# The first batch of an attention-then-MoE kernel: another order of its steps, and unused matmuls on TensorE between them

## The chip, the cores and the metric

The kernel runs on one core of a Trainium2 chip. A core has five engines, each with its own in-order instruction stream: TensorE (PE, matmul; PEld is its weight load), VectorE (DVE), ScalarE (ACT), GpSimd (POOL) and SyncE (SP, which here only issues DMAs). They wait for one another through semaphores. Matmuls read SBUF and write PSUM, which has eight banks per partition. The metric is the device time of one execution in microseconds (us); lower is better. Runs of one kernel are compared by their median.

## The reference

```python
rms = np.sqrt(np.mean(x * x, axis=-1, keepdims=True) + 1e-06)      # rmsnorm(x, g)
return x / rms * g
...
q_n, k_n = (rmsnorm(q, g_q), rmsnorm(k, g_k))
scores = scale * np.matmul(q_n, k_n.transpose(0, 1, 3, 2))
scores = scores - np.max(scores, axis=-1, keepdims=True)
attn = np.exp(scores)
attn = attn / (np.sum(attn, axis=-1, keepdims=True) + 1e-09)
return np.matmul(attn, v)
...
x = attn_out.transpose(0, 2, 1, 3).reshape(B * S, H * D)
h = x @ w_in
g = np.maximum(0.01 * h, h)
return g @ w_out
```

q, k and v are 8 x 12 x 448 x 64 in fp32 (batch, heads, sequence, head dimension); w_in is 768 x 2048, w_out 2048 x 768. The output is 3584 x 768.

## The kernel before, in words

**Units.** A unit is four heads of one batch, so there are 24 units (`NU`), three to a batch (`NQ`). A unit's sequence of 448 is cut into seven steps (`NS`) of 64 keys, for two heads (`a`) by two heads (`r`).

**Preparation of a unit.** `load` puts q and k into raw tiles through SP (three buffers), `load_v` puts v into one of five tiles through GpSimd's queue, which also carries the weights (`load_w_in`, `load_w_out`). Squares come from ScalarE (`prep_sq`, L126) or GpSimd (`prep_sqp`, L130), q times g from GpSimd (`prep_qg`, L134), the sums of squares from VectorE (`prep_ssq`, L139), the inverse root from ScalarE (`prep_rinv`, L144 and L145), the normalised tiles from VectorE (`prep_norm`, L151). The transposed q and k (`qkT`) come from 14 TensorE transposes and two copies out of PSUM (`prep_tr`, L159 and L160) for units 0 to 4, and from a DMA transpose on SP's queue (`prep_trd`, L163) from unit 5 on. `gate` (L229) is a small GpSimd copy that waits for the normalised k and so holds GpSimd's later work.

**Scores and exponentials.** `qk` computes the scores of a step with four matmuls into one of two two-bank slots (`sT`, L179); `ex` applies the exponential on ScalarE (L198, for step 0 from `score0` L196). All rows of a unit share one shift per partition, taken from the maximum of step 0: `shift_max` (L211 to L218, VectorE) finds the maximum and writes it on a diagonal, `shift_mm` (L223 to L226) spreads it by a matmul with ones and makes `eb`, the bias of the exponentials. So a unit's first exponential waits for scores, maximum, diagonal, matmul, maximum and `eb` in turn.

**Z and PV.** In the first batch `zsum` (L238) sums the exponentials by 28 matmuls with ones, `pv` (L309) multiplies them with v by 28 matmuls; `zinv` (L295 to L300) makes the inverse of Z as exp(-ln Z) on ScalarE, `xmul` (L318) multiplies on VectorE into `xt`, the MoE's input. `zsum_slot` puts Z into one of the two score slots. The remaining accumulators, transposes and small banks take turns in four PSUM banks (`aux`): a new tile waits until the readers of the one four tiles earlier are done.

**MoE.** `moe1` (L324, L326) computes one of 16 blocks of h from six matmuls and applies the leaky ReLU on ScalarE; `moe2` (L339, L343) computes the output. They are put in a queue when a batch's attention is complete, and `fill` deals them out between the steps of the later units, from unit 3 on. The order is written out by hand (a manual schedule): what stands first in the program stands first on its engine.

**The head.** The first batch (units 0 to 2) has no MoE work to lay between its steps. Ahead of unit 0 stand 60 unused matmuls (`warm`, L401), 128 x 128 with ones, in two groups. The loop over `u in range(3)` (L457 to L523) then does, for each unit: `ex` of step 0; `zinv` of the unit before; norm of the next unit; sum of squares of the one after; loads; steps 1 and 2, 3 and 4, 5, 6 with their exponentials; transposes of the next unit; step 0 of the next unit and its shift; Z and PV. Unit 2 does Z and PV of steps 0 to 4 together after step 6, then those of steps 5 and 6.

Of the kernel before, what the change touches and what calls it, by code (L numbers as in the profile page):

```python
# [8 lines left out]
FP32 = mybir.dt.float32  # L9
# [9 lines left out]
def kernel(  # L19
# [11 lines left out]
    nc = tc.nc  # L31
# [3 lines left out]
    NS = 7  # L35
    P = 128
# [18 lines left out]
    def aux(shape, dtype, name):  # L55
        return psum.tile(shape, dtype, tag="aux", bufs=4, name=name)
# [36 lines left out]
    st = {}  # L93
# [111 lines left out]
    def shift_max(u):  # L205
# [11 lines left out]
        s["dg"] = small.tile([P, P], FP16, tag="dg", name="dg")  # L217
        nc.vector.tensor_tensor(s["dg"], ident16, s["spare"][:, 511:512].broadcast_to([P, P]), op=ALU.mult)  # L218

    def shift_mm(u):  # L220
        s = st[u]
        pb = aux([P, 512], FP32, "pb")
        nc.tensor.matmul(pb[:, 0:P], onesp, s["dg"], start=True, stop=True)  # L223
        nc.vector.tensor_reduce(s["spare"][:, 510:511], pb[:, 0:P], axis=AXL.X, op=ALU.max)
        s["eb"] = small.tile([P, 1], FP32, tag="eb", name="eb")
        nc.vector.tensor_scalar(s["eb"], s["spare"][:, 510:511], -1.0, DELTA, op0=ALU.mult, op1=ALU.add)  # L226

    def gate(u):
        nc.gpsimd.tensor_copy(gate_t, buf(u, "n16")[:, 1, NS - 1, 1, D - 1:D])  # L229
# [166 lines left out]
    K0, K1 = (0, 1), (1, NS)  # L396
    VV = ((ALL, vcopy),)

    def warm(n):
        for x in range(n):  # L400
            nc.tensor.matmul(wbank[:, 0:P], onesp, onesp, start=True, stop=True)  # L401

    with tc.manual_schedule():
        nc.scalar.dma_start(grow[:, 0], g_q[None, :])
        nc.scalar.dma_start(grow[:, 1], g_k[None, :])
        nc.scalar.preload_act_table_set("natural_log_exp_and_others")
        load(0)
        load(1)
        load(2)
        gps = aux([P, 512], FP32, "gps")  # L410
        wbank = aux([P, 512], FP32, "warm")
        warm(32)
        nc.vector.scalar_tensor_tensor(grow[:, 0], grow[:, 0], 0.125, grow[:, 1], op0=ALU.mult, op1=ALU.mult)
        nc.tensor.matmul(gps[:, 0:D], one32, grow[:, 0], start=True, stop=True)
        warm(28)
        prep_sq(0, CA, (0,))
        prep_sq(0, CB, (0,))
        acopy(ggb, gps[:, 0:D])
        prep_sq(0, ALL, (1,))
        prep_qg(0, nc.gpsimd, CA)  # L420
        prep_qg(0, nc.gpsimd, CB)
        prep_ssq(0, CA, (0,))
        prep_ssq(0, CB, (0,))
        prep_rinv(0, (0,))
        prep_ssq(0, ALL, (1,))
        prep_rinv(0, (1,))
        prep_sq(1, ALL, (0,))
        load_v(0)
        load_v(1)
        prep_norm(0, CA, (0,))  # L430
        prep_norm(0, CB, (0,))
        prep_tr(0, 0, ((CA, acopy), (CB, acopy)))
        prep_norm(0, K0, (1,))
        prep_norm(0, K1, (1,))
        tpk = aux([P, NS, P], FP16, "tp")

        def trk(c, copy):
            for x in range(*c):
                nc.tensor.transpose(tpk[:, x, :], buf(0, "n16")[:, 1, x].rearrange("p a d -> p (a d)"), ident16)
            copy(buf(0, "qkT")[:, 1, c[0]:c[1]], tpk[:, c[0]:c[1]])  # L440

        trk(K0, vcopy)
        prep_ssq(1, ALL, (0,))
        qk(0, STEPS[0])
        prep_sq(1, ALL, (1,))
        trk(K1, acopy)
        prep_sq(2, ALL, (0,))
        load(3)
        gate(0)
        prep_qg(1, nc.gpsimd)  # L450
        prep_sqp(2, (1,))
        shift_max(0)
        shift_mm(0)
        load_w_in(0, 1024)
        load_v(2)

        for u in range(3):  # L457
            n = u + 1
            ex(u)
            if u == 0:  # L460
                prep_ssq(n, ALL, (1,))
                prep_rinv(n)
            else:
                zinv(u - 1)
            prep_norm(n)
            prep_ssq(u + 2)
            load(u + 4)
            gate(n)
            prep_qg(u + 2, nc.gpsimd)
            prep_sqp(u + 3)  # L470
            load_v(u + 3)
            if u == 0:
                load_w_in(1024, 1024)
            if u == 1:
                for f in range(2):
                    load_w_out(8 * f, 8)
            qk(u, STEPS[1])
            ex(u)
            if u > 0:
                prep_tr(n, 0, VV)  # L480
                prep_tr(n, 1, VV)
                xmul(u - 1)
            qk(u, STEPS[2])
            ex(u)
            if u == 0:
                prep_tr(n, 0, VV)
            qk(u, (5,))
            ex(u)
            prep_rinv(u + 2)
            if u == 0:  # L490
                prep_tr(n, 1, VV)
                qk(u, (6,))
                ex(u)
                score0(n)
                shift_max(n)
                shift_mm(n)
            elif u == 1:
                score0(n)
                shift_max(n)
                qk(u, (6,))  # L500
                ex(u)
                shift_mm(n)
            else:
                qk(u, (6,))
                ex(u)
            if u < 2:
                zsum_slot(u)
                pv(u)
            else:
                st[u]["zt"] = [aux([P, 512], FP32, "zt") for r in range(2)]  # L510
                zsum(u, 0, 5)
                pv(u, 0, 5)
                qk(n, STEPS[0])
                zsum(u, 5, NS)
                pv(u, 5, NS)
                zinv(u)
                shift_max(n)
                xmul(u)
                push_moe1(0)
                push_moe2(0)  # L520
                queue.pop(0)[1]()
                shift_mm(n)
                ex(n)  # L523

        for u in range(3, NU):
            for d in range(4):
                if d > 0 or u > 3:
                    qk(u, STEPS[d])
                    if d == 0:
                        shift_max(u)  # L530
                        if narrow(u - 1):
                            pv_slot(u - 1)
                            zcol(u - 1)
                            shift_mm(u)
                            pv_out(u - 1)
                            zcol_sum(u - 1)
                        else:
                            zsum_slot(u - 1)
                            pv(u - 1)
                            shift_mm(u)  # L540
                            zinv(u - 1)
                    ex(u)
                jobs = []

                def job(fn, *args):
                    jobs.append(lambda: fn(*args))

                if d == 0:
                    if u == 3:
                        prep_norm(4)  # L550
                        gate(4)
                    elif narrow(u - 1):
                        job(zcol_inv, u - 1)
                    else:
                        xmul(u - 1)
                    if u + 4 < NU:
                        job(load, u + 4)
                    if u + 2 < NU:
                        prep_qg(u + 2, nc.gpsimd)
                    if u + 3 < NU:  # L560
                        load_v(u + 3)
                    if 6 < u < NU - 2:
                        for ti in range(2):
                            job(prep_sq, u + 2, ALL, (ti,))
                if d == 1 and u > 3 and narrow(u - 1):
                    xmul_pool(u - 1)
                if fed(u, d) and u > 3:
                    push_moe1(u // NQ - 1)
                    push_moe2(u // NQ - 1)
                if u < 6 and d == 2:  # L570
                    prep_sqp(u + 3)
                if u == 3 and d == 1:
                    for ti in range(2):
                        prep_tr(4, ti, VV)
                if u + 2 < NU:
                    if d == 1:
                        for ti in range(2):
                            job(prep_ssq, u + 2, ALL, (ti,))
                    if d == 2:
                        job(prep_rinv, u + 2)  # L580
                        for ti in range(2):
                            job(prep_norm, u + 2, ALL, (ti,))
                        job(prep_trd, u + 2)
                fill(u, d, jobs)
        zsum_slot(NU - 1)
        pv(NU - 1)
        zinv(NU - 1)
        xmul(NU - 1)
        push_moe1(B - 1)
        push_moe2(B - 1)  # L590
        while queue:
            queue.pop(0)[1]()
# [28 lines left out]
```

## Time and profile before

| | us |
|---|---|
| median of six runs | 449.02 |
| the six runs | 449.88, 449.85, 447.74, 448.19, 450.05, 447.77 |
| profiled execution | 447.45 |
| its span, first to last instruction | 445.7 |

The page of the profile gives each engine's busy time in the span: PE 417.9 us (94%), ACT 306.6 (69%), DVE 215.9 (48%), POOL 148.2 (33%). The mean granted TensorE clock is 0.984. In lists of instructions a line gives start, duration, engine, source line, operation, tiles (out<-in), and in brackets how long the engine had been idle and who ended the wait. A wait for several events is put down to the last. `PEclk` is the granted clock, 1.00 for full speed. The span's first 48 us are the head and the start of unit 3.

### The profile page before, as it was taken

How to read it: one execution, taken by the hardware profiler on the slowest of the kernel's cores; microseconds unless marked ns; L12 is line 12 of the kernel's file. 1: busy time of each engine (PE TensorE's matmuls, PEld its weight loads, DVE VectorE, ACT ScalarE, POOL GpSimd, SP SyncE). 2: the span in 40 equal slices, each digit the busy share in tenths (PEclk: the TensorE clock that was granted, in tenths of full speed). 3: DMA queues.
4: the chain of work that ended last, by engine and by line, in shares of the span. 5: the costliest groups of instructions: out<-in, count | busy, mean ns of one | idle time of the engine just before them, and what ended most of it. 6: DMA issues, size and time to landing. Idle time of an engine off the chain costs nothing.

```text
span 445.7 us, 8599 instructions
## 1 busy us (share of the span) xinstructions
PE 417.9 (94%) x3608; PEld 212.7 (48%) x3608; DVE 215.9 (48%) x320; ACT 306.6 (69%) x458; POOL 148.2 (33%) x102
## 2 busy tenths in 40 slices
PE   5668999999999999999999999999999999999995
PEld 5234444444445544454445544454455544555563
DVE  5886664875435735555345734545446521120021
ACT  5888788577886498787886598776995677634300
POOL 5896563643413413523512413423511110100000
PEclk9599999999999999999999999999999999999999
DMA  8999999589547855587558784586443550211022
GB/s 276 241 249 254 225 157 181 162 170 215 117 129 143 212 162 96 135 214 145 125 139 109 197 210 65 144 203 153 131 79 78 124 107 1 60 54 37 0 72 71
DMA packets 67979, 62.81 MB, mean 141 GB/s; under 512 B 37477, under 2 KB 62821, under 8 KB 67941
## 3 DMA queue, kind: packets, MB, share of 16 engines
q1 hardware_dynamic: 57664, 50.47, 45.6%
q0 software_dynamic: 10272, 11.80, 17.6%
q8 instruction: 28, 0.46, 0.4%
q14 instruction: 11, 0.08, 0.0%
q10 hardware_dynamic: 4, 0.00, 0.0%
HBM read 45.61 MB, written 11.01 MB: 127 GB/s over the span
## 4 chain that ended last, share of the span: by engine, by line
PE 75%; ACT 16%; DVE 5%; DMA 2%; issue 1%; SPq 0%; DVEq 0%; ACTq 0%
PE op L339 31%; PE hps L324 24%; ACT et L198 7%; PE sT L179 7%; PE sT L309 5%; PE zc L255 3%; ACT sq L126 3%; ACT gt L326 3%; DMA rq<-in_q_dram 2%; PE sT L238 1%; DVE n L151 1%; ACT zs L278 1%; PE pb L223 1%; PE pv L309 1%; ACT zs L277 1%
## 5 line engine op out<-in xcount | busy, mean ns | idle before, releaser
L198 ACT ACTIVATE et<-sT,eb 128x896 f16<-128x896 f32 x166 | 158.9, 1006 | 37.5 <-PE sT L179 26.4
L324 PE MATMUL hps<-xt,win 128*128 128x448 f16 x768 | 153.8, 353 | 1.3 <-DVE xt L318 1.0
L339 PE MATMUL op<-wout,gt 128*128 128x384 f16 x896 | 153.8, 326 | 0.4 <-ACT gt L326 0.4
L339 PEld LDWEIGHTS <-gt 128*128 128x128 f16 x896 | 84.7, 98 | 66.5 <-issue 12.5
L324 PEld LDWEIGHTS <-win 128*128 128x128 f16 x768 | 72.0, 98 | 72.1 <-issue 10.3
L289 POOL TENSOR_TENSOR xt<-x,rz 128x896 f16<-128x896 f32 x19 | 39.6, 2084 | 182.3 <-DMA rz<-zs 98.3
L326 ACT ACTIVATE gt<-hps 128x448 f16<-128x448 f32 x128 | 67.0, 546 | 21.4 <-PE hps L324 20.9
L343 DVE COPY ost<-op 128x384 f32<-128x384 f32 x56 | 31.2, 556 | 95.2 <-PE op L339 91.3
L134 POOL TENSOR_TENSOR qg<-rq,ggb 128x896 f32<-128x896 f32 (+2 forms) x25 | 60.3, 2415 | 45.6 <-DVE n L151 41.5
L139 DVE TENSOR_REDUCE ssq<-sq 128x14 f32<-128x896 f32 (+2 forms) x49 | 50.3, 1060 | 30.3 <-ACT sq L126 30.3
L179 PE MATMUL sT<-qkT 64*64 64x448 f16 x664 | 54.2, 372 | 10.6 <-ACT et L198 9.6
L151 DVE TENSOR_TENSOR n<-qg,rinv 128x896 f16<-128x896 f32 (+2 forms) x25 | 27.4, 1100 | 41.4 <-issue 26.7
L267 ACT COPY x<-sT 128x896 f32<-128x896 f32 x19 | 17.2, 906 | 38.4 <-PE sT L309 38.4
L179 PEld LDWEIGHTS <-qkT 64*64 64x64 f16 x672 | 16.2, 105 | 47.4 <-issue 43.0
L216 DVE TENSOR_REDUCE sT<-sT 128x1 f32<-128x896 f32 x22 | 24.1, 1094 | 27.2 <-PE sT L179 27.2
L151 DVE TENSOR_TENSOR n<-rk,rinv 128x896 f16<-128x896 f32 (+2 forms) x25 | 33.2, 1330 | 0.0
L309 PE MATMUL sT<-et,vt 64*64 64x448 f16 x532 | 28.4, 349 | 0.3 <-ACT et L198 0.3
L309 PEld LDWEIGHTS <-vt 64*64 64x64 f16 x672 | 20.2, 107 | 10.9 <-issue 0.9
L126 ACT ACTIVATE sq<-rq 128x896 f32<-128x896 f32 (+2 forms) x19 | 17.0, 901 | 2.0 <-DMA rq<-in_q_dram 2.0
L106 POOL DMA_DIRECT2D vt<-in_v_dram x24 | 18.3, 763 | 0.0
L255 PE MATMUL zc<-et,onesr 128*32 128x448 f16 (+1 forms) x304 | 16.1, 332 | 0.0
L126 ACT ACTIVATE sq<-rk 128x896 f32<-128x896 f32 x17 | 16.0, 939 | 0.1
(60 smaller groups left out, 197.5 us busy)
## 6 DMA issues: line engine op xcount, KB each, us to landing
rq<-in_q_dram SPq DMA_DIRECT2D x24, 448.0 KB, 4.8
rk<-in_k_dram SPq DMA_DIRECT2D x24, 448.0 KB, 5.8
out_dram<-ost SPq DMA_DIRECT2D x56, 192.0 KB, 2.8
rz<-zs SPq DMA_DIRECT2D x38, 224.0 KB, 3.5
vt<-in_v_dram POOLq DMA_DIRECT2D x24, 224.0 KB, 5.1
win<-in_moe_w_in_dram POOLq DMA_DIRECT2D x8, 384.0 KB, 14.3
wout<-in_moe_w_out_dram POOLq DMA_DIRECT2D x2, 1536.0 KB, 27.0
qkT<-n SPq DMA_TRANSPOSE x19, 4.0
```

What stands on the lines that cost most here:

```text
L126: nc.scalar.activation(buf(u, "sq")[:, ti, :, c[0]:c[1]], raw[u][ti][:, :, c[0]:c[1]], AF.Square)
L134: eng.tensor_tensor(buf(u, "qg")[:, :, c[0]:c[1]], raw[u][0][:, :, c[0]:c[1]], ggb[:, None, None, :].broadcast_to([P, 2, n, D]), op=ALU.mult)
L139: nc.vector.tensor_reduce(buf(u, "ssq")[:, ti, :, c[0]:c[1]], buf(u, "sq")[:, ti, :, c[0]:c[1]], axis=AXL.X, op=ALU.add)
L151: nc.vector.tensor_tensor(buf(u, "n16")[:, ti, c[0]:c[1]].rearrange("p s a d -> p a s d"), src[:, :, c[0]:c[1]], buf(u, "rinv")[:, ti, :, ...
L179: nc.tensor.matmul(banks[a][64 * r:64 * r + 64, 0:S].rearrange("p (t x) -> p t x", t=NS), kT(u, r, a, t), qT(u, r, a), start=True, stop=True)
L198: nc.scalar.activation(s["et"][:, t], sT[:, :, 0:S], AF.Exp, bias=s["eb"], scale=1.0)
L289: nc.gpsimd.tensor_tensor(xts[b][:, g], s["x32"], s["rz"], op=ALU.mult)
L309: nc.tensor.matmul(s["pv"][r][64 * a:64 * a + 64, 0:S], vts[u % NV][64 * r:64 * r + 64, a, t], s["et"][64 * r:64 * r + 64, t, a], start=(t ...
L324: nc.tensor.matmul(hps[:, 0:S], win16[:, kt // 2, kt % 2, ts(ft, P)], xt[:, kt // 2, kt % 2], start=(kt == 0), stop=(kt == KT - 1))
L326: nc.scalar.activation(gt[:, ft, ds(S * (b % 2), S)], hps[:, 0:S], AF.Prelu, bias=0.0, scale=1.0, alpha=0.01)
L339: nc.tensor.matmul(op2[:, 0:HC], gt[:, ft, ts(t, P)], wout16[:, ft, ds(HC * half, HC)], start=(ft == 0), stop=(ft == FT - 1))
L343: nc.vector.tensor_copy(ost[0][:, ds(HC * half, HC)], op2[:, 0:HC])
```

## The change

- `shift_mm`'s PSUM bank can be taken earlier (`shift_bank`), and `warm` writes into any bank; 12, 20 and 6 unused matmuls go into the second quarter of the shift banks of units 0, 1 and 2, ahead of the shift matmul. 16, 12 and 6 more stand behind steps 1, 2 and 3 of unit 0.
- The loop over the first three units is written out. A unit's end (`close`, units 0 and 1) is Z, the exponential of step 0 of the next unit, its step 1 of QK, PV, and `zinv`. Before, step 1 of QK stood behind PV, with step 2.
- Unit 0: transposes of unit 1 stand together behind step 4, the second copied by ScalarE (before: apart, behind steps 4 and 5, both copied by VectorE). `prep_rinv(2)` moves from behind step 5 to behind step 6.
- Unit 2: Z and PV are accumulated as steps come: 0 to 2 after the exponential of step 4, 3 after step 5, 4 after step 6, then step 0 of unit 3, then 5 and 6 (before: 0 to 4 after step 6). `prep_rinv(4)` moves behind step 6, `prep_ssq(4)` behind the transposes of unit 3 and `xmul(1)`.

From unit 3 on the program is the same.

```diff
+    def shift_bank(u):
+        st[u]["pb"] = aux([P, 512], FP32, "pb")
+
     def shift_mm(u):
         s = st[u]
-        pb = aux([P, 512], FP32, "pb")
+        if "pb" not in s:
+            shift_bank(u)
+        pb = s["pb"]
...
-    def warm(n):
+    def warm(n, bank):
         for x in range(n):
-            nc.tensor.matmul(wbank[:, 0:P], onesp, onesp, start=True, stop=True)
+            nc.tensor.matmul(bank[:, P:2 * P], onesp, onesp, start=True, stop=True)
...
         shift_max(0)
+        shift_bank(0)
+        warm(12, st[0]["pb"])
         shift_mm(0)
         load_w_in(0, 1024)
         load_v(2)
 
-        for u in range(3):
...
+        def feed(u):
             load(u + 4)
-            gate(n)
+            gate(u + 1)
             prep_qg(u + 2, nc.gpsimd)
             prep_sqp(u + 3)
             load_v(u + 3)
...
+        def trn(u, ti, copy):
+            prep_tr(u, ti, ((ALL, copy),))
+
+        def sums(u, t0, t1):
+            zsum(u, t0, t1)
+            pv(u, t0, t1)
+
+        def close(u):
+            n = u + 1
+            zsum_slot(u)
+            ex(n)
+            qk(n, (1,))
+            pv(u)
+            zinv(u)
+
+        ex(0)
+        prep_ssq(1, ALL, (1,))
+        prep_rinv(1)
+        prep_norm(1)
+        prep_ssq(2)
+        feed(0)
+        load_w_in(1024, 1024)
+        wb = aux([P, 512], FP32, "warm")
+        qk(0, (1,))
+        ex(0)
+        warm(16, wb)
+        qk(0, (2,))
+        ex(0)
+        warm(12, wb)
+        qk(0, (3,))
+        ex(0)
+        warm(6, wb)
+        qk(0, (4,))
+        ex(0)
+        trn(1, 0, vcopy)
+        trn(1, 1, acopy)
+        qk(0, (5,))
+        ex(0)
+        qk(0, (6,))
+        ex(0)
+        prep_rinv(2)
+        score0(1)
+        shift_max(1)
+        shift_bank(1)
+        warm(20, st[1]["pb"])
+        shift_mm(1)
+        close(0)
+
+        prep_norm(2)
+        prep_ssq(3)
+        ex(1)
+        feed(1)
+        for f in range(2):
+            load_w_out(8 * f, 8)
+        qk(1, (2,))
+        ex(1)
+        trn(2, 0, vcopy)
+        trn(2, 1, vcopy)
+        xmul(0)
+        qk(1, (3, 4))
+        ex(1)
+        qk(1, (5,))
+        ex(1)
+        prep_rinv(3)
+        score0(2)
+        shift_max(2)
+        qk(1, (6,))
+        ex(1)
+        shift_bank(2)
+        warm(6, st[2]["pb"])
+        shift_mm(2)
+        close(1)
+
+        prep_norm(3)
+        ex(2)
+        feed(2)
+        qk(2, (2,))
+        ex(2)
+        trn(3, 0, vcopy)
+        trn(3, 1, vcopy)
+        xmul(1)
+        prep_ssq(4)
+        qk(2, (3,))
+        ex(2)
+        qk(2, (4,))
+        ex(2)
+        st[2]["zt"] = [aux([P, 512], FP32, "zt") for r in range(2)]
+        sums(2, 0, 3)
+        qk(2, (5,))
+        ex(2)
+        sums(2, 3, 4)
+        qk(2, (6,))
+        ex(2)
+        prep_rinv(4)
+        sums(2, 4, 5)
+        qk(3, STEPS[0])
+        sums(2, 5, NS)
+        zinv(2)
+        shift_max(3)
+        xmul(2)
+        push_moe1(0)
+        push_moe2(0)
+        queue.pop(0)[1]()
+        shift_mm(3)
+        ex(3)
```

The removed lines of the loop are those of L457 to L523 above.

More of the change, by code (lines that the diff above doesn't have):

```diff
@@ L411 @@
         wbank = aux([P, 512], FP32, "warm")
-        warm(32)
+        warm(32, wbank)
         nc.vector.scalar_tensor_tensor(grow[:, 0], grow[:, 0], 0.125, grow[:, 1], op0=ALU.mult, op1=ALU.mult)
         nc.tensor.matmul(gps[:, 0:D], one32, grow[:, 0], start=True, stop=True)
-        warm(28)
+        warm(28, wbank)
         prep_sq(0, CA, (0,))
@@ L455 @@
         load_v(2)
-        for u in range(3):
[L458 to L466, printed above, removed]
+        def feed(u):
             load(u + 4)
-            gate(n)
+            gate(u + 1)
             prep_qg(u + 2, nc.gpsimd)
@@ L471 @@
             load_v(u + 3)
[L472 to L523, printed above, removed]
+        def trn(u, ti, copy):
+            prep_tr(u, ti, ((ALL, copy),))
```

## The prediction

> **What bounds the kernel now.** I read the busy shares first, then five stages by the clock stretches, then ScalarE's list up to the first MoE matmuls, then the chain of waits and the DMA answers.
>
> ```profile
> PE 417.9 (94%) x3608; PEld 212.7 (48%) x3608; DVE 215.9 (48%) x320; ACT 306.6 (69%) x458; POOL 148.2 (33%) x102
> ```
>
> TensorE bounds the kernel as a whole, but not its head. The stages say where it doesn't (columns: stretch, length, busy time of PE, PEld, DVE, ACT, POOL, then PEclk, DMA share, GB/s):
>
> ```profile
> 7.50:11.20 3.70, 0.82 (x12) 0.67 (x12) 2.68 (x6) 2.46 (x6) 3.08 (x5) 1.00 1.05 392
> 11.20:21.50 10.30, 7.00 (x53) 3.04 (x52) 8.68 (x12) 9.42 (x14) 9.14 (x10) 0.50 1.10 240
> 21.50:31.70 10.20, 6.12 (x103) 3.47 (x100) 9.32 (x16) 7.83 (x11) 10.20 (x11) 1.00 1.13 249
> 31.70:35.10 3.40, 2.80 (x29) 1.27 (x32) 2.94 (x8) 2.50 (x6) 2.98 (x4) 0.50 1.14 238
> 35.10:48.00 12.90, 9.74 (x143) 5.60 (x136) 7.70 (x14) 10.72 (x16) 6.23 (x5) 1.00 1.13 247
> ```
>
> Up to 48 us ScalarE, VectorE and GpSimd are fuller than TensorE; from 49 to 61.3 us TensorE is busy for 11.75 of 12.30 us, from 91 to 130 for 38.54 of 39. So a microsecond won in the head moves all that follows, unless something later is tied to a clock of its own. The reader also sees two half-clock stretches, 10.3 and 3.4 us. What the head loses stands in ScalarE's brackets:
>
> ```profile
> 19.55 1.01 ACT L198 ACTIVATE et<-sT,eb 128x896 f16<-128x896 f32 x1 [0.28 <-PE sT L179]
> 24.27 1.16 ACT L196 ACTIVATE et<-s,eb 128x448 f16<-128x448 f32 x2 [2.34 <-DVE eb L226]
> 35.35 0.92 ACT L295 ACTIVATE rz<-sT 128x896 f32<-128x896 f32 x1 [1.06 <-PE sT L238]
> 43.77 0.54 ACT L299 ACTIVATE rz<-zt 128x448 f32<-128x448 f32 x1 [0.67 <-PE zt L238]
> 47.06 0.54 ACT L326 ACTIVATE gt<-hps 128x448 f16<-128x448 f32 x1 [1.10 <-PE hps L324]
> ```
>
> These are 5.45 us of gaps; elsewhere between 13 and 48 us ScalarE runs through. The 2.34 us is the shift chain of unit 1 (two copies, scores, two maxima, diagonal, matmul, eb); the 1.06 us is Z of unit 1 at half clock:
>
> ```profile
> 23.57 1.52 PE L238 MATMUL sT<-et,ones 64*64 64x448 f16 x28
> 32.50 2.80 PE L238 MATMUL sT<-et,ones 64*64 64x448 f16 x28
> ```
>
> **The change part by part**, against the profiled execution: 447.45 us, span 445.7 and 1.75 around it.
>
> *Unused matmuls.* 72 are added (12+16+12+6+20+6). Their price is in the first microseconds:
>
> ```profile
> 1.16 3.49 PE L401 MATMUL warm<-onesp 128*128 128x128 f16 x32 [1.16 <-DVE onesp L67]
> 4.95 1.74 PE L401 MATMUL warm<-onesp 128*128 128x128 f16 x28
> ```
>
> 109 ns each in the first 3.4 us, 62 ns after: slow and full clock. The first 12 go between the last six transposes (from 11.64) and the shift matmul, in the half-clock stretch: 18 x 0.109 from 11.64 is 13.60, where the shift matmul starts at 13.28 now. So eb and ex of unit 0 come later by **+0.32** (0 if the clock is full there, 0.5 if each pair drains first; I take the issue row). The 16 start about 14.2. The busy stretch that 18.07 to 21.48 is now (after it the clock is full) then lies at 11.2 to 14.65, so the clock should be full from 14.65. The 16 end about 15.4, where step 2 waits for ex 0 anyway; the 12 and 6 (0.75 and 0.37 us) fit in the 0.92 us that each ex takes. The 20 (1.24 us) run while VectorE does 1.9 us of maxima and diagonal, the 6 before dg of unit 2. If that cover went, each group would cost its own length.
>
> *Unit 0's end.* Both transposes now follow step 4 and the second copy goes from VectorE (0.62) to ScalarE (0.80 us for 768 columns, so 0.93). VectorE is back to back from rinv at 15.68 through norms and sums to the copies' end at 21.02; with one copy less, scores of unit 1 start 0.62 sooner, and take 0.38 instead of 0.56 at full clock: **-0.80**. ScalarE pays the 0.93 and rinv of unit 2 (0.57), moved behind ex 6, inside its 2.34 us gap: its work ends at about 23.0, eb comes at 23.8. Cover gone (a gap below 1.5 us), they would be on the path. Norm 2 on VectorE is next behind rinv 2 and needs it at 23.7. So ex of unit 1 starts 0.48 sooner, 23.8.
>
> *Second QK step before PV.* Four matmuls (0.19 us of issue) ahead of 28. ScalarE goes from rz (26.27, 0.95 long) into ex at 27.12 with no gap now, and at 37.16 likewise: **0**; PV comes 0.2 later, its reader xmul waits for the tp copies long after.
>
> *Unit 1.* VectorE and ScalarE run without a gap from eb, so all moves by 0.48 to Z of unit 1. Does the clock fall there? Cut into single microseconds, the granted clock changes at about 11.24, 21.48, 31.72 and 35.14, all multiples of 3.41 us apart, so I count TensorE's busy time in such windows. In 28.31 to 31.72 TensorE was busy 1.57 us and the clock fell after it; in 38.55 to 41.96 it was busy 1.82 and kept it. The same steps plus 6 fillers (0.37) make about 1.95. I take full clock: Z 1.5 us, done at 33.3 before ScalarE frees at 33.85, and the **-1.06** gap goes. Bounds: 0 and -1.06. The Trainium skill, "TensorE: Matmul & The Clock Gate", HAM oscillation, speaks against this: its rule is to avoid TensorE gaps longer than about 3.4 us. The longest gap before 31.7 is 0.52 us and the clock fell all the same, so the trace decides; by the rule the fillers would buy nothing here and the sum would lack this term: 447.1 instead of 446.0.
>
> *Unit 2.* rinv of unit 4 moves behind ex 6, so Z's last step (0.57) runs beside it: from ex at 37.16 to 43.77 is 6.61 us now, 6 x 0.92 + 0.57 = 6.09 after: **-0.52**. ssq of unit 4 moves behind copies and xmul of unit 1 on VectorE: done about 40.3, needed 41.5. But the first Z group now stands before step 5 in TensorE's queue, and its banks are those that xmul 1 reads (ends about 38.3): 12 Z and 12 PV matmuls (0.048 each, 1.1 us) then hold step 5 until 39.35, ready for ScalarE at 39.75 instead of 39.45: **+0.30** (0 to 1.2, if xmul slips). V of unit 2, issued 16.58 and landed after 16.1 us, is there by 32.7.
>
> *Queues.* The loads on SP and GpSimd stand in the same order as before; only the time shifts. GpSimd runs full from 18.0 to 34.7, its gate waits for norm 1, 0.3 later. w_in's second half lands at 46.5, needed after 50.
>
> *The DMA transpose of unit 5*, the next to be late:
>
> ```profile
> 71.63 0.38 PE L179 MATMUL sT<-qkT 64*64 64x448 f16 x4 [0.29 <-DMA qkT<-n]
> ```
>
> It is issued at 58.56, right after norm 5, and TensorE waits for its landing 13 us later; later ones land in 4.0 to 5.0 us. DMA share is over 1 from 11 to 72 us. If the landing is fixed by the backlog, all the gain goes here; if it moves with its issue, nothing. In 61.5 to 62, beside weights still moving, its queue passed 92 packets in 0.5 us; alone, from 65 to 68, some 170 in 1 us. So sharing doesn't slow it, and an earlier start should carry over: **+0.3** of a possible 1.7.
>
> Sum: 0.32 - 0.80 - 1.06 - 0.52 + 0.30 + 0.3 = -1.46, so 446.0 for such an execution.
>
> **To the median.** The six times are two groups, 447.74 to 448.19 and 449.85 to 450.05; the profiled one belongs to the first, 0.32 under its middle: 446.3. What makes the second group no trace shows; I guess half-clock stretches falling elsewhere, which fillers should shorten, and allow 0.2: **446.5 us**. The same page (What's actually happening) says that the clock's window runs freely and doesn't restart with a kernel; no trace here shows that.
>
> **Rivals.**
> - *The transpose holds the gain.* For it: the saturated share; against: the packet rates. The gain stops at its 0.28: 447.2 to 447.8.
> - *Half clock in unit 1 stays.* 1.95 us may be too little. Loses 1.06: 447.1, with the transpose and the second group 447.0 to 448.3.
> - *Slower: the fillers don't lift the clock in unit 0.* Then steps are held by them: 16 take 1.75 us and 12 take 1.31, QK 0.59; step 3 comes at 18.75 instead of 17.8, step 4 another 0.35 late, 14 transposes 1.53 for 0.87, the shift matmul 0.3, Z 1.3, less the copy's 0.62: +3.3 with the first 0.32. This gives 450.7, without Z 449.4; it decides once the clock stays down past about 18. Against it: 32 in a row lifted the clock after 3.4 us at the start.
> - *No change in effect*: the old gaps reappear as others, 449.
>
> **How the numbers follow.** Main case 0.55 (444.9 to 447.3; the lower end is no DMA loss, no 0.30, first 0.32 zero), transpose 0.14, half clock 0.11, slower 0.10, no change 0.10. Within 0.3% of 449.02, which a measurement can just tell, is 447.67 to 450.37. Faster: 0.55 + most of 0.25 = 0.73; within: 0.18; slower: 0.09. The range leaves out the slower case and half of no change: 444.9 to 449.2.
>
> **What would show it.** PEclk near 1 from 15 us on; ex of unit 1 at 23.8; no gap before rz of unit 1, Z in 1.5 us; rz of unit 2 at 42.0; the sixth matmul of the first MoE group at about 45 (46.68 now); TensorE's wait on qkT near 70 under 0.6. Wrong if 0.50 stands in PEclk after 18 us, if that wait is over 1.5, or if step 5 of unit 2 is over 1 us late.

## The result, and the profile after

The changed kernel takes 445.93 us (median of 22 runs, 443.95 to 447.45) against 449.06 us of the kernel before (46 runs, 447.48 to 450.96). The ratio is 0.9925 with a 95% interval of 0.9913 to 0.9936: 0.75% faster. A later repetition of 12 runs on another chip gave 0.9949 (0.9932 to 0.9966). The profiled execution took 445.09 us with a span of 443.3, so it is 2.36 us under that of before and 0.84 us under its own median.

The stages by the granted clock, as of before (stretch, length, busy time of PE, PEld, DVE, ACT, POOL, PEclk, DMA share, GB/s):

```profile
7.50:10.80 3.30, 0.78 (x8) 0.53 (x8) 2.40 (x6) 2.17 (x5) 2.69 (x5) 0.98 1.04 388
10.80:14.50 3.70, 3.40 (x33) 2.64 (x34) 2.93 (x7) 2.85 (x5) 3.38 (x3) 0.56 1.16 263
14.50:27.20 12.70, 10.58 (x169) 7.36 (x167) 11.10 (x16) 11.50 (x17) 11.63 (x16) 1.00 1.06 241
27.20:30.60 3.40, 1.63 (x20) 0.58 (x19) 3.24 (x7) 3.40 (x5) 3.40 (x2) 1.00 1.16 240
30.60:48.00 17.40, 14.08 (x202) 8.07 (x199) 12.81 (x22) 15.77 (x25) 11.14 (x12) 1.00 1.13 242
```

One half-clock stretch of one window is left, against 10.3 and 3.4 us before. ScalarE's list in the head (start, duration, idle before it in brackets; a line without brackets follows at once):

```profile
14.40 1.01 ACT L198 ACTIVATE et<-sT,eb 128x896 f16<-128x896 f32 x1 [0.27 <-DVE eb L231]
23.73 1.16 ACT L196 ACTIVATE et<-s,eb 128x448 f16<-128x448 f32 x2 [1.11 <-DVE eb L231]
33.59 0.92 ACT L300 ACTIVATE rz<-sT 128x896 f32<-128x896 f32 x1
41.45 0.54 ACT L304 ACTIVATE rz<-zt 128x448 f32<-128x448 f32 x1
44.74 0.54 ACT L331 ACTIVATE gt<-hps 128x448 f16<-128x448 f32 x1 [1.10 <-PE hps L329]
```

The gap before unit 1 fell from 2.34 to 1.11 us (ScalarE now does the second copy, 0.92 us, and rinv of unit 2 ahead of it), those before rz of unit 1 (1.06) and of unit 2 (0.67) are gone, the last is as it was. On TensorE the shift matmul of unit 0, Z of unit 1, the sixth matmul of the first MoE block, and the scores of unit 5 with their wait:

```profile
13.52 0.31 PE L228 MATMUL pb<-dg,onesp 128*128 128x128 f16 x1
31.90 1.52 PE L243 MATMUL sT<-et,ones 64*64 64x448 f16 x28
44.35 0.35 PE L329 MATMUL hps<-xt,win 128*128 128x448 f16 x1 [0.69 <-DVE xt L323]
69.81 0.38 PE L179 MATMUL sT<-qkT 64*64 64x448 f16 x4 [0.80 <-DMA qkT<-n]
```

The sixth MoE matmul stood at 46.68 us, so the head is 2.33 us shorter. After the wait on the transpose the lead is 2.27 us (shift matmul of unit 5 at 72.23 instead of 74.50), and at the last unit's 2.34 (375.40 for 377.74). What the head won reached the end.

### The profile page after: what moved, and what is told of

The parts are those of the page before. It is cut to its first block, busy times and chain, and to the rows that moved or that the text cites. A ratio compares the mean times of both kernels' runs of the same rounds, so it can differ in the third digit from the quotient of the medians.

```text
span 443.3 us, 8743 instructions
## 1 busy us (share of the span) xinstructions
PE 419.1 (95%) x3680; PEld 216.2 (49%) x3680; DVE 215.4 (49%) x319; ACT 307.1 (69%) x459; POOL 148.0 (33%) x102
## 4 chain that ended last, share of the span: by engine, by line
PE 72%; ACT 16%; DVE 5%; DMA 5%; issue 1%; SPq 0%; DVEq 0%; ACTq 0%
PE op L344 31%; PE hps L329 23%; ACT et L198 7%; PE sT L179 7%; PE sT L314 5%; PE zc L260 3%; DMA qkT<-n 3%; ACT sq L126 2%; ACT gt L331 2%; DVE n L151 2%; DMA rq<-in_q_dram 2%; ACT zs L283 1%; PE pb L228 1%; ACT zs L282 1%; DVE sT L229 1%
## 5 line engine op out<-in xcount | busy, mean ns | idle before, releaser
L314 PEld LDWEIGHTS <-vt 64*64 64x64 f16 x672 | 20.1, 107 | 10.3
```

The lines of the kernel that those rows point to most:

```text
L314: nc.tensor.matmul(s["pv"][r][64 * a:64 * a + 64, 0:S], vts[u % NV][64 * r:64 * r + 64, a, t], s["et"][64 * r:64 * r + 64, t, a], start=(t ...
```

## The experiments

Every kernel ran beside the kernel before on its chip. "Against before" is the difference of the means, with a 95% interval from resampling the runs; the changed kernel itself has -3.37 us (-3.84 to -2.92) beside its own 46 runs of before, and -2.29 (-2.91 to -1.63) in the later repetition. Differences of less than 1 us between kernels of 6 to 12 runs are therefore not settled by the times alone. Where that matters, the length of a stretch inside the profiles is given beside them.

### The new order without the fillers, and the fillers without the new order

```diff
-        warm(12, st[0]["pb"])
...
-        wb = aux([P, 512], FP32, "warm")
...
-        warm(16, wb)
...
-        warm(12, wb)
...
-        warm(6, wb)
...
-        warm(20, st[1]["pb"])
...
-        warm(6, st[2]["pb"])
```

> The changed kernel without its 72 unused matmuls; all else of the new order stays. Theory (the clock is worth its own part): the two half-clock stretches come back, about 11.2 to 21.5 and 31.7 to 35.1 us; ScalarE again waits about 1 us before rz of unit 1 and Z of unit 1 takes 2.8 us; ex of unit 0 starts at 14.1 (0.3 sooner), ex of unit 1 at about 23.6. Median 1.0 to 2.0 us over the changed kernel's 445.9, so 447 to 448, with a spread as wide as before's 3.5 us. Rival (the new order did it, the fillers buy nothing): 445.9 within 0.4.

Measured: 447.30 us (12 runs, 446.52 to 448.15), -1.32 us against before (-1.73 to -0.91). The mean granted clock of its runs is 0.979 to 0.983, as before's; the runs spread over 1.63 us, not over the 3.5 expected. In its profile, stages and the two rz:

```profile
12.30:26.00 13.70, 9.22 (x82) 4.05 (x85) 11.17 (x18) 10.62 (x16) 13.52 (x16) 0.50 1.05 239
26.00:32.10 6.10, 4.08 (x66) 2.19 (x59) 4.75 (x9) 6.07 (x8) 6.10 (x6) 1.00 1.16 258
32.10:36.00 3.90, 3.50 (x41) 1.85 (x44) 2.78 (x6) 2.94 (x6) 2.53 (x5) 0.60 1.10 258
```

```profile
25.51 0.92 ACT L300 ACTIVATE rz<-sT 128x896 f32<-128x896 f32 x1 [1.03 <-PE sT L243]
35.35 0.92 ACT L300 ACTIVATE rz<-sT 128x896 f32<-128x896 f32 x1 [0.91 <-PE sT L243]
```

Here the half clock lasted from 12.4 until 26 us, so that Z of unit 0 was slow too: 1.03 us before the first rz, 0.91 before the second. The next kernel is the one before with the 72 fillers at the same places:

```diff
+                for t, n_w in ((1, 16), (2, 12), (3, 6)):
+                    qk(0, (t,))
+                    ex(0)
+                    warm(n_w, wb)
...
+                warm(20, st[n]["pb"])
...
+                warm(6, st[n]["pb"])
```

> The kernel before with the 72 unused matmuls at the same places and nothing else changed (the steps of unit 0 are issued one by one so that the fillers can stand between; the order on each other engine is that of before). Theory: gains the 1.06 us at Z of unit 1 and 0.2 at the scores of unit 1, loses 0.3 at the first shift: 1 us under before, about 448.0, a little more at the median if before's slow executions are those with more half clock (down to 447). Rival (fillers do all): 446. Rival (fillers only help with the new order): 449. The granted clock should be full from 14.7 us in this one in either case.

Measured: 447.91 us (12 runs, 445.58 to 448.37), -1.11 us (-1.65 to -0.63); mean clocks of 0.989 to 0.996. Order and fillers are worth about as much, and their sum (-2.43) lies within what the changed kernel itself showed (-2.29 to -3.37), so neither rival holds. The third expectation, a full clock from 14.7 us on, failed: in this profile it fell at 22.4 us and again at 32.7,

```profile
32.10:36.00 3.90, 3.51 (x38) 1.69 (x41) 3.53 (x7) 2.77 (x6) 2.51 (x5) 0.57 1.11 260
```

and rz of unit 1 again waited 1.08 us for Z.

### Step 1 of QK behind PV again

```diff
             ex(n)
+            pv(u)
             qk(n, (1,))
-            pv(u)
             zinv(u)
```

> The changed kernel with step 1 of QK of units 1 and 2 behind PV again, as before; all else changed. Theory: nothing, 445.9 within 0.3, since ScalarE goes from rz into ex without a gap in both profiles and PV ends 0.7 us before rz. Rival (this is a part of the gain that I did not see): 0.5 us or more slower, with a gap before the first ex behind rz.

Measured: 445.92 us (12 runs), the changed kernel's own median; -2.67 us against before (-3.37 to -1.86). This part of the change is worth nothing that these runs can tell.

### Unit 2's Z and PV together again

```diff
-        st[2]["zt"] = [aux([P, 512], FP32, "zt") for r in range(2)]
-        sums(2, 0, 3)
         qk(2, (5,))
         ex(2)
-        sums(2, 3, 4)
         qk(2, (6,))
         ex(2)
         prep_rinv(4)
-        sums(2, 4, 5)
+        st[2]["zt"] = [aux([P, 512], FP32, "zt") for r in range(2)]
+        sums(2, 0, 5)
```

> The changed kernel with Z and PV of steps 0 to 4 of unit 2 together behind step 6, as before; rinv of unit 4 stays behind step 6. Theory: 24+24 matmuls less 8 stand on the path again behind step 6 (QK at 40.1, Z 0.95, PV 0.95, QK 0.2, Z 0.4): rz of unit 2 starts at about 43.0 instead of 41.5, so 1.3 to 1.6 us slower, 447.3; part of it can be hidden if the transpose of unit 5 gave back time (its wait falls from 0.8 to 0.3): then 447.0. Rival (the stepwise sums only move idle time, rinv in the gap was all): within 0.5 of 445.9.

Measured: 447.13 us (12 runs), -1.58 us against before (-2.16 to -0.98), and 1.1 us slower (0.15 to 1.9) than the run above on the same chip. From rz of unit 1 to the sixth matmul of the first MoE block the profile has 11.32 us, that of before 11.33 and that of the changed kernel 10.76, so 0.56 us belong to the sums (the half clock before has no part in it: TensorE waited 0.52 us for ScalarE ahead of steps 5 and 6); where the rest comes from isn't shown. ScalarE waits at Z of unit 2 again, as long as in the kernel before, although rinv now stands before it, so moving rinv alone brought nothing:

```profile
34.04 0.92 ACT L300 ACTIVATE rz<-sT 128x896 f32<-128x896 f32 x1 [1.09 <-PE sT L243]
42.46 0.54 ACT L304 ACTIVATE rz<-zt 128x448 f32<-128x448 f32 x1 [0.67 <-PE zt L243]
```

The first line is the second lesson of this run: all six fillers of unit 1 are there, and the clock still fell, at about 28.3 us, and stayed down over Z of unit 1:

```profile
28.30:35.10 6.80, 6.33 (x63) 3.07 (x66) 4.49 (x9) 5.22 (x9) 6.71 (x7) 0.50 1.12 264
```

```profile
31.16 2.83 PE L243 MATMUL sT<-et,ones 64*64 64x448 f16 x28
```

### The copy on VectorE, and the first twelve fillers

```diff
-        trn(1, 1, acopy)
+        trn(1, 1, vcopy)
```

> The changed kernel with the second copy of unit 1's transposes on VectorE again; all else changed. Theory: scores of unit 1 start 0.62 us later and so does all behind them, ScalarE's gap before ex of unit 1 grows from 1.1 to 2.6 (it has 0.93 less to do): 446.4 to 446.6 against 445.9. Rival (the copies are off the path, the earlier scores come from the clock): 445.9 within 0.3.

Measured: 446.63 us (6 runs), 0.7 us over the changed kernel's first 22 runs and 0.45 over its later 12, which six runs don't settle. The profile is clearer: from ex of unit 0 to ex of unit 1 it has 9.87 us, both profiles of the changed kernel 9.32 to 9.33, so the copy is worth 0.54 us (expected 0.62). ScalarE's gap is back to what it was with both copies on VectorE:

```profile
24.24 1.16 ACT L196 ACTIVATE et<-s,eb 128x448 f16<-128x448 f32 x2 [2.44 <-DVE eb L231]
```

The 12 fillers ahead of unit 0's shift matmul, which I had priced at 0.32 us, were taken out alone:

```diff
         shift_bank(0)
-        warm(12, st[0]["pb"])
         shift_mm(0)
```

> The changed kernel without the 12 unused matmuls ahead of unit 0's shift matmul. Theory: the shift matmul starts 0.25 to 0.32 us sooner where the clock is half there, ex of unit 0 follows at once behind the squares; but the clock comes up one window of 3.41 us later in some executions, which costs little as ScalarE runs full there: 445.6 to 446.0. Rival (these 12 are needed to lift the clock): 446.5 or more and a mean clock under 0.990.

Measured: 446.65 us (7 runs, 445.30 to 448.45), mean clock 0.985 to 0.991: the rival, by both of its signs, though the runs overlap with the changed kernel's. The shift matmul does start at once, but the clock comes up at 17.9 us instead of 14, and until then the 16 and 12 fillers behind it take 1.89 and 1.46 us instead of 1.07 and 0.84 and hold the steps that stand behind them:

```profile
14.03 1.89 PE L406 MATMUL warm<-onesp 128*128 128x128 f16 x16
15.85 0.59 PE L179 MATMUL sT<-qkT 64*64 64x448 f16 x4
16.37 1.46 PE L406 MATMUL warm<-onesp 128*128 128x128 f16 x12
17.76 0.42 PE L179 MATMUL sT<-qkT 64*64 64x448 f16 x4
```

```profile
18.24 1.91 ACT L198 ACTIVATE et<-sT,eb 128x896 f16<-128x896 f32 x2 [0.73 <-PE sT L179]
```

This is the mechanism of the prediction's slower rival, one window long. From ex of unit 0 to ex of unit 1 it costs 0.51 us (9.84 for 9.33). In the 11 profiles that have all fillers of unit 0 the half clock that begins near 11 us lasts one window of 3.41 us or doesn't come; here it lasts two, in the kernel before three, without fillers four.

### More fillers: before 10 us, and as repeated scores in unit 1

```diff
-        warm(28, wbank)
+        warm(40, wbank)
...
-        prep_tr(0, 0, ((CA, acopy), (CB, acopy)))
+        tpq = aux([P, NS, P], FP16, "tp")
+        for lo, hi in (CA, CB):
+            for x in range(lo, hi):
+                nc.tensor.transpose(tpq[:, x, :], buf(0, "n16")[:, 0, x].rearrange("p a d -> p (a d)"), ident16)
+            acopy(buf(0, "qkT")[:, 0, lo:hi], tpq[:, lo:hi])
+            if lo == 0:
+                warm(24, wbank)
```

> The changed kernel with 40 unused matmuls for 28 after the first small matmul and 24 more between the two groups of transposes of unit 0's q, so that TensorE is busy from 1 to 10 us. Theory: the clock isn't lost at 11 us, so scores, six transposes, 12 fillers and the shift matmul of unit 0 run at full clock: ex of unit 0 starts 0.4 to 0.6 us sooner, 445.4, and the mean clock rises by 0.005 to 0.008. Rival (the clock there costs nothing, squares on ScalarE hold ex of unit 0): 445.9.

Measured: 445.73 us (6 runs); mean clock 0.995 to 0.998, a rise as expected, but the time is within what the runs scatter. In its profile ex of unit 0 came at 14.22 us, not 0.4 to 0.6 us sooner. Part of that is a later start, since ScalarE waited 0.50 us for k at 6.1 us: from the diagonal (dg) to ex of unit 0 it has 1.12 us, the changed kernel 1.51 in its first profile and 1.17 in its second, so the clock there is worth 0.05 to 0.39 us. The clock was full through the first 30 us and fell at 30.7, with 0.90 us before rz of unit 1.

```diff
-    def qk(u, steps):
+    def qk(u, steps, times=1):
...
-            score(u, t, (sT[:, 0], sT[:, 1]))
+            for x in range(times):
+                score(u, t, (sT[:, 0], sT[:, 1]))
...
-        qk(1, (3, 4))
+        qk(1, (3, 4), 3)
...
-        qk(1, (5,))
+        qk(1, (5,), 2)
...
-        qk(1, (6,))
+        qk(1, (6,), 2)
```

> The changed kernel with the scores of steps 3 and 4 of unit 1 computed three times and those of 5 and 6 twice, into the same slot, as fillers in the one stretch of the head that has none. Theory (the fillers of the changed kernel don't hold the clock in all executions; when it falls between 27 and 32 us, Z and PV of unit 1 pay about 1 us): the slower executions go, the median falls by 0.4 to 0.6 to 445.4, the mean clock rises to 0.996 or more. Rival (the spread has another cause, such as the loads): median and spread as now, 445.9 and 0.95, with a higher clock.

Measured: median 445.27 us, 6 of 7 runs between 444.50 and 445.93, one of 448.90; mean clocks mostly 0.994 to 0.995, under the 0.996 expected. The repeated scores have a price: from ex of unit 1 to ex of unit 2 the profile has 9.08 us, the changed kernel's 8.81. The run of 448.90 was the profiled execution, and it shows the rival that the prediction named for the transpose of unit 5, at full size:

```profile
56.68 1.40 SPq L163 DMA_TRANSPOSE qkT<-n  x1
```

```profile
71.86 0.38 PE L179 MATMUL sT<-qkT 64*64 64x448 f16 x4 [2.39 <-DMA qkT<-n]
72.08 2.51 PE L315 MATMUL sT<-et,vt 64*64 64x448 f16 x28
74.51 1.47 PE L261 MATMUL zc<-et,onesr 128*32 128x448 f16 x16
```

The landing came 15.2 us after the issue. TensorE stood for 2.39 us, and then PV took 2.51 instead of 1.49 and Z 1.47 instead of 0.85: the granted clock fell at 72.4 us. The shift matmul was 1.87 us ahead of before's in unit 4 and 1.41 behind in unit 5: 3.3 us in one place. In no other of the 14 profiles does this stretch, from the shift of unit 4 to that of unit 5, differ by more than 0.05 us from before's 13.16.

### v one unit later, the changed kernel again, and all together

```diff
-            load_v(u + 3)
+            if u < 2:
+                load_v(u + 3)
...
-                    if u + 3 < NU:
-                        load_v(u + 3)
+                    if u + 2 < NU:
+                        load_v(u + 2)
```

> The changed kernel with v of units 5 and up loaded one unit later, so that two loads of v (0.9 MB read) leave the weights' queue before 62 us; all else changed. Theory (the landing of unit 5's DMA transpose depends on what stands in the DMA engines, so it is the next thing to be late in the faster head): it lands 11 us or less after its issue (13.5 and 15.2 in two profiles with a wait), TensorE's wait for it is 0, the slowest executions go, median 445.4 to 445.7. Rival (the landing is the transpose's own time): the same wait, 445.9. Rival (v comes late itself): a wait for v in PV of unit 5 and more than 446.5.

Measured: 446.03 us (6 runs), and in the profile the same wait:

```profile
55.95 1.40 SPq L163 DMA_TRANSPOSE qkT<-n  x1
69.37 0.38 PE L179 MATMUL sT<-qkT 64*64 64x448 f16 x4 [0.63 <-DMA qkT<-n]
```

13.4 us from the issue to the scores that waited for it, with two loads of v fewer before it. The 11 us of my theory didn't come: in this profile it isn't these loads.

> The changed kernel itself on this chip, as the reference for the two others: 445.9 within 0.4, with a spread of 444 to 447.5 that follows the granted clock (lower clock, longer time).

Measured: 446.18 us (12 runs, 444.85 to 448.30), mean clock 0.987 to 0.995. Its profile has no wait on the transpose at all (issued 56.03, scores at 68.85 without a wait), so with one and the same kernel the landing takes at most 12.8 us in one execution and 13.6 in another. The profiled execution took 445.88 us, 0.79 more than the first one of this kernel, though its shift matmul of unit 5 came 0.25 us sooner (71.98 for 72.23). The place where it lost is later:

```profile
95.67 3.03 POOL L294 TENSOR_TENSOR xt<-x,rz 128x896 f16<-128x896 f32 x1 [6.11 <-DMA rz<-zs]
98.75 0.54 PE L329 MATMUL hps<-xt,win 128*128 128x448 f16 x2 [0.74 <-POOL xt L294]
```

TensorE waited for GpSimd's multiplication, which took 3.03 us instead of the 2.07 of the first profile.

> The changed kernel with the fillers before 10 us, the repeated scores in unit 1 and v one unit later. Theory: the clock is full in nearly every execution (mean 0.998 or more) and the transposes of unit 5 are there in time: 444.6 to 445.0, spread under 1.5 us. Rival (what the clock gives, waits of GpSimd's and VectorE's shared stretches take back): 445.4 or more with the same high clock.

This kernel has the early fillers, the repeated scores and the later v, by the diffs above. Measured: 444.95 us, all 6 runs within 444.82 to 445.44, mean clock 0.997 to 1.000; 1.22 us under the changed kernel's runs on the same chip (interval 0.68 to 1.80), ratio to before 0.9922 (0.9904 to 0.9940). It has the lowest median of the kernels here. Its stages:

```profile
5.00:14.00 9.00, 6.70 (x108) 5.79 (x108) 7.22 (x14) 6.54 (x14) 7.72 (x8) 1.00 1.08 326
14.00:27.00 13.00, 10.44 (x167) 7.22 (x165) 11.40 (x16) 11.80 (x18) 12.37 (x16) 1.00 1.08 239
27.00:31.00 4.00, 3.30 (x50) 1.70 (x50) 3.55 (x8) 3.97 (x7) 4.00 (x3) 1.00 1.16 249
31.00:35.00 4.00, 3.50 (x69) 1.98 (x69) 2.89 (x6) 3.76 (x6) 4.00 (x6) 1.00 1.13 259
```

> The kernel of the run before without the later loads of v: the changed kernel with the fillers before 10 us and the repeated scores in unit 1. Theory (the steadier clock alone made the gain, as the later v alone changed neither median nor wait): 445.0 within 0.4, spread under 1.5 us. Rival (the later v is what keeps the transpose of unit 5 in time when all else is early): 445.5 or more, with single executions over 446.5 as the one of 448.9 with the repeated scores, and a wait on qkT in the profile.

Without the later v: 445.26 us (6 runs, 444.87 to 446.97), mean clock as high. Between the two lies no difference that six runs show. The spread of 2.1 us is wider than the 1.5 expected and one run is over the rival's 446.5, so the rival isn't excluded. Against before this kernel has -3.32 us, no more than the changed kernel's first -3.37, so that the further gain of the steadier kernels rests on the chip of the repetition. Its profiled execution, 445.88 us, had no wait on the transpose but the one on GpSimd, which the profile of the kernel with all three doesn't have:

```profile
95.78 1.08 DVE L151 TENSOR_TENSOR n<-rk,rinv 128x896 f16<-128x896 f32 x1
95.85 2.95 POOL L295 TENSOR_TENSOR xt<-x,rz 128x896 f16<-128x896 f32 x1 [6.19 <-DMA rz<-zs]
98.85 0.54 PE L330 MATMUL hps<-xt,win 128*128 128x448 f16 x2 [0.74 <-POOL xt L295]
```

In the changed kernel's first profile the two instructions start the other way round, GpSimd 0.03 us before VectorE:

```profile
95.91 2.07 POOL L294 TENSOR_TENSOR xt<-x,rz 128x896 f16<-128x896 f32 x1 [6.10 <-ACT et L198]
95.94 2.99 DVE L151 TENSOR_TENSOR n<-rk,rinv 128x896 f16<-128x896 f32 x1
```

It is VectorE's that is stretched, and nothing waits. The one that starts later by a few hundredths pays, GpSimd 0.9 us or VectorE 1.9, and only GpSimd's is on the path. TensorE's wait stands in 4 of the 14 profiles, and these take 0.9 us more from the shift of unit 5 to the last one (304.1 for 303.2).

### The clock in unit 1, over all profiles

Nine profiles have the six fillers of unit 1 without repeated scores. In six of them the clock fell between 28.3 and 32.7 us; it held in both of the changed kernel and in that with v later, and in all three with repeated scores. In each profile I split time into windows of 3.41 us, laid so that the clock's changes fall on their ends, and took TensorE's busy time (the number behind the length). The three windows below are from the changed kernel, after which the clock held, and from the copy on VectorE and step 1 of QK behind PV, after which it fell:

```profile
27.70:31.11 3.41, 2.06 (x26) 0.90 (x26) 3.25 (x7) 3.41 (x5) 3.41 (x3) 1.00 1.17 242
29.33:32.74 3.41, 1.95 (x31) 1.00 (x30) 2.77 (x7) 3.38 (x6) 3.41 (x3) 1.00 1.13 255
26.15:29.56 3.41, 1.57 (x20) 0.61 (x20) 3.24 (x6) 3.41 (x5) 3.41 (x3) 1.00 1.15 259
```

Of the windows at full clock that begin between 4 and 80 us, in the 12 profiles where the clock changes, all 13 with at most 1.61 us of TensorE time were followed by half clock and all with more than 2.0 us by full clock; of the 16 in between, ten kept it and six lost it. The same steps and fillers fall on either side, by where the window divides them.

## Why the prediction was right

The forecast was 446.5 us within 444.9 to 449.2, faster at 0.73; measured 445.93, faster. By its steps:

- **First fillers, +0.32.** Right in size for this profile: the shift matmul moved by 0.24 us (13.28 to 13.52), ex of unit 0 by 0.29. In the second profile of the same kernel the stretch from the diagonal to ex of unit 0 was 1.17 us, as before, so there the term was zero. The clock came up at 14.05 us, 0.6 sooner than forecast. And the term is no cost that could be saved: without these 12, unit 0 took 0.51 us more.
- **The second copy and the scores, -0.80, -0.48 with the first term.** Right: ex of unit 1 at 23.73 (predicted 23.8), 0.54 us sooner. From ex of unit 0 to ex of unit 1 it takes 9.33 us for 10.16, so -0.83. The copy alone undone cost 0.54 us of that (predicted 0.62).
- **QK before PV, 0.** Right.
- **Unit 1's clock, -1.06.** Right for the profiled execution, where Z took 1.52 us and the gap went, but by luck of where the window lay. I took 1.95 us of TensorE time in a window of 3.41 us for enough, because 1.82 had kept the clock. In this profile the window had 2.06 us; with 1.95 the clock fell in two other profiles, and it fell in six of the nine with these fillers. So the fillers hold the clock in some executions only, and the runs' mean clock (0.988 to 1.000) follows the time with a correlation of -0.74.
- **Unit 2, -0.52 and +0.30.** The stretch is right for the first term (from ex behind rz of unit 1 to rz of unit 2 6.61 us became 6.06), but its cause isn't: I gave the gain to rinv's move and counted the stepwise sums as a cost, and with rinv moved and the sums together nothing was gained. The sums carry the gain; whether they would without rinv's move was not run. The second is the term that failed. I had step 5 of QK held by the Z group until 39.35, because the group waits for xmul's banks until 38.3. But xmul ended at 37.88, the group started at 37.52, and step 5 ran at 38.65 without ScalarE waiting:

```profile
36.73 1.15 DVE L323 TENSOR_TENSOR xt<-pv,rz 128x448 f16<-128x448 f32 x2
37.52 0.76 PE L243 MATMUL zt<-et,ones 64*64 64x448 f16 x12
38.65 0.39 PE L179 MATMUL sT<-qkT 64*64 64x448 f16 x4
```

The head came out 0.57 us shorter (2.33) than predicted (1.76): 0.35 of it in unit 2, 0.22 before rz of unit 1. The hold that I feared does exist where the clock is lost: with the copy on VectorE, at half clock until 36.2 us, PV's group waited 0.15 us for xmul and ScalarE then 0.60 for the scores of step 5.

- **The transpose, +0.3.** Too large: the wait grew from 0.29 to 0.80 us, over the 0.6 that I had named, but PV behind it no longer waited for ScalarE and started 0.22 us after the scores instead of 0.65, so the lead shrank by 0.06 only. The landing, by the scores that waited for it, moved by 1.82 us with 2.33 of its issue, so it mostly moves along. Later transposes land in 4.0 to 7.1 us in the profile of before, not in 5.0 at most. What decides the landing stays open: v later changed nothing, and equal kernels differ.
- **To the median.** Here the reading was wrong. With 46 runs, the times of before are no two groups; they spread evenly over 3.5 us, in part with the clock (correlation -0.70 over 35 runs, -0.16 to -0.76 on three other chips). The allowance of +0.2 went the wrong way: the medians differ by 3.13 us, the profiled executions by 2.36. The runs show why it could be so, not that it must: the fillers cut the lost clock of all executions to about a third (mean 0.979 to 0.993), and the profiled execution of before, 0.984, had less to lose than most. The closeness of the median is in part luck: the profiled execution came 0.9 us under its sum (445.09 for 446.0), and the median 0.84 over it where I had allowed 0.5.

Of the rivals, "half clock in unit 1 stays" was true of a part of the executions, "the transpose holds the gain" of one profile with repeated scores, and the slower one showed itself where the fillers start too late (without the first 12).

The clock's dependence on where the window lies could be seen in this case after all: the half clock began at 11.24 us in the profile of before and at 10.64 in that of after, at 12.38 in that without fillers, with the work before it unchanged. This agrees with what the Trainium skill ("TensorE: Matmul & The Clock Gate", What's actually happening) says of a window that runs freely and doesn't restart with the kernel. Its other rule that I weighed, no TensorE gap longer than about 3.4 us, is again not enough in these traces: with unit 2's sums together the clock fell at 28.3 us with a longest gap of 0.52.

## What to carry to other kernels

Unused matmuls between the steps of a stretch that another engine bounds are worth trying, where they fit into TensorE's gaps: here 72 were worth 1.1 us in the old order and 1.35 in the new (no fillers against step 1 of QK behind PV, on one chip), and the steadiest version 1.2 more on the one chip where it ran beside the changed kernel. They must be dense enough for every position of the clock's window, not only for that of one profile: here more than 2.0 us of TensorE time in every 3.41 us held the clock, and the repeated scores, which kept it so in unit 1, cost 0.27 us. The first of them must come early, since fillers that run at half clock hold the work behind them. Take sums out of the end of a dependent chain by accumulating as the parts arrive (0.56 us here by the profiles, 1.1 by the runs). Judge such changes by the spread of many runs, since one profile shows one position of the window, one order of two engines that start 0.03 us apart, and one start: ex of unit 0 came at 13.23 to 13.45 us in the four profiles where the second q tile was there in time, and at 13.88 to 14.57 in the ten where ScalarE waited 0.5 to 1.1 us for q or k.

## What the runs showed of the hardware

- The granted clock steps at multiples of 3.41 us, at another offset in each execution. It is one cause of the spread among several: the same kernel spread over 3.5 us; with a mean clock of 0.997 to 1.000 one kernel spread over 0.6 us in six runs and another over 2.1.
- At full clock, in these profiles, windows of 3.41 us with at most 1.61 us of TensorE time were all followed by half clock and those with more than 2.0 us by full clock.
- A single wait of 2.39 us on a DMA, in a window with 1.02 us of TensorE time, was followed by matmuls at half speed, which cost 1.6 us on top.
- A DMA transpose that lands in 4.0 to 7.1 us later in the kernel (median 4.0) takes 13.1 to 15.2 us in the stretch where the weights load where it was waited for, and at most 12.8 in another execution of the same kernel.
- When GpSimd's multiplication and VectorE's normalisation overlap, the one that starts later takes longer, 2.95 for 2.07 us or 2.99 for 1.08, and the first keeps its length. Both fit the Trainium skill, "SBUF — State Buffer", SBUF: two separate sides, which has the two engines take a shared pair of ports as an exclusive lock: in the second case VectorE's instruction ends at 95.94 + 2.99 = 98.93 us, 0.95 after GpSimd's end at 95.91 + 2.07 = 97.98, which is about its length alone (1.08); in the first GpSimd's ends at 98.80, 1.94 after VectorE's end at 96.86, about its 2.07.
